# First chunk of the projections: q and k row tile by row tile in one loop, their last 64 rows side by side

## The chip, the cores and the metric

The kernel runs on one core of one Trainium2 chip. A core has five engines that run on their own and wait for one another by semaphores: TensorE (PE, matmuls; PEld is its weight load, which overlaps the matmuls), VectorE (DVE), ScalarE (ACT), GpSimd (POOL) and SyncE (SP), which here issues the DMA transfers. Each engine runs its own instructions in the order in which they were written. Matmuls accumulate in PSUM banks; other data lie in SBUF, 128 partitions wide. The metric is the device time of one execution in microseconds (us). The profiled execution is a single one with the hardware profiler on; its rows give the start and length of each instruction in us from the start of the span.

## The reference

One sequence of S = 2048 tokens with D = 448 features goes through two branches, which a gate mixes per token:

```python
x = A_x
g = _sigmoid((x * gate_w).sum(-1, keepdims=True))
a = _A_ref(x, A_wqkv, A_wo)                  # attention
b = _B_ref(x, B_w1, B_b1, B_w2, B_b2)        # relu(x @ w1 + b1)**2 @ w2 + b2
return g * a + (1 - g) * b
```

The attention has 16 heads of 28 features. Each token looks at eight keys, those 0, 2, ..., 14 places before it (`W, dil = 8, 2`), with a softmax over the eight; q, k and v are the three thirds of `x @ wqkv`. All data are float32. Only the first projections, `x @ wqkv` for a quarter of the tokens, are touched by the change.

## The kernel before, in words

**Precision by three products.** TensorE works on a shortened float32 (`fp32r`). Each operand is therefore split into a high part, rounded by a copy on ACT, and a low part, the rest, by a subtraction on DVE (`split_full`, lines 113 to 115). A product is the sum of three matmuls: high by high, high by low, low by high.

**Tiling.** The 448 rows of the contraction are three row tiles of 128 and a last one of 64 (`w7h`, `w7l`, `x.x7`, `x.x8` hold the last one; it stands in both halves of the partitions, the upper half of its weights being q's and the lower half k's). A chunk is 512 tokens, four token tiles of 128. An accumulator (`Acc`) is one PSUM bank with 128 tokens by 448 columns (450 for q, whose columns 448 and 449 are the gate's). It needs 9 full matmuls (three row tiles by three products) and three half matmuls for the last 64 rows. Alternatively a full matmul can be cut into two halves of 64 rows; `side_by_side` issues two such halves, of two different accumulators, on the two halves of the array, and a pair takes as long as one full matmul. An accumulator that goes from one half of the array to the other needs a small write to its bank in between, a turn, by DVE or ACT (`turn`, lines 191 to 199).

**Banks.** There are eight PSUM banks, four under the tag "b" and four under "m", each tag given out in rotation. In the first chunk q's four accumulators take the "b" banks, k's the "m" banks, and v's again the "b" banks.

**The first chunk, `qkv_first` (line 257).** Before the change it does, in this order on TensorE: for each of the three row tiles the 12 full matmuls of q (3 products, 4 token tiles); then 48 pairs of halves, in which q's last 64 rows run beside k's last 64 rows (12 pairs) and then k's full row tiles run as halves of two token tiles (36 pairs); then v in 42 pairs. Between the pairs stand turns and evacuations. A call of `run` takes two lists of halves and a list of steps (up to which pair, which accumulators are then complete, which turns).

**Evacuation, `qkv_evacuate` (line 201).** ACT copies the bank into a stage tile in SBUF (line 207). A stage tile holds two neighbouring token tiles of one of q, k or v; the pool has `ST_BUFS = 3` of them in rotation under one tag. When the second half is in, SP stores the stage tile to DRAM with one DMA of 448 KB (line 213). For q, ACT also copies the gate's column (line 215). A stage buffer can be given out again when its store is complete.

**Loads at the start (lines 635 to 652).** SP issues, for each row tile, q's weights and x; then the last 64 rows; then k's three row tiles and v's. Each row tile is split on ACT and DVE (lines 653 to 667), first q's weights and x, then the last 64 rows, then k's weights (lines 711 and 712).

**The order of the rest.** The kernel is written in one order by hand. A model clock (`advance`, `at`, `when`) counts the planned time of the matmuls that were emitted, and emits work that falls due: v's weight splits at 12,000 ns and after, the store of the split x to DRAM (`x_spill`, line 139) at 10,500, the splits of chunk 1's x from 19,000, the next x loads, and so on. In what order such work and the evacuations stand on ACT, DVE and SP follows from how far the clock was moved at that point. The next chunks use `qkv_two`; attention on POOL, DVE and ACT and the second branch follow.

Of the kernel before, what the change touches and what calls it, by code (L numbers as in the profile page):

```python
# [7 lines left out]
F32 = mybir.dt.float32  # L8
# [5 lines left out]
S, D, H, DH, W, F = 2048, 448, 16, 28, 8, 1792  # L14
P = 128
# [8 lines left out]
NQ = D + 2  # L24
# [7 lines left out]
MM448 = 203.0  # L32
# [25 lines left out]
def gated_mix_kernel(ctx: ExitStack, tc: tile.TileContext, xT, wqkv, w1, w2, wo, b1, b2, out):  # L58
    nc = tc.nc

    def f32(ap):
        return ap.bitcast(F32)
# [29 lines left out]
    attp = ctx.enter_context(tc.tile_pool(name="attp", bufs=1))  # L92
# [20 lines left out]
    def split_full(raw, hi, lo, soon=now):  # L113
        nc.scalar.activation(hi, raw, AF.Copy)
        soon(lambda: nc.vector.tensor_sub(lo, raw, f32(hi)))

    def split_x78(raw, x7, x8, soon=now):

        split_full(raw, x7, x8, soon)
# [12 lines left out]
    def x_tiles(c, pool):  # L132
        return X([pool.tile([P, 2, CH], F32R, tag=f"x{j}", name=f"x{c}_{j}") for j in range(4)])
# [19 lines left out]
    wqh = ap.tile([P, 3, NP + 2 * D], F32R, name="wqh")  # L153
    wql = ap.tile([P, 3, NP + 2 * D], F32R, name="wql")
# [10 lines left out]
    def ncols(b):  # L165
        return NQ if b == 0 else D

    def block(b):

        o = (0, NP, NP + D)[b]  # L170
        return slice(o, o + ncols(b))
# [8 lines left out]
    def side_by_side(*todo):  # L180


        assert len(todo[0]) == len(todo[1])
        for pair in zip(*todo):
            for r, (acc, a, w) in enumerate(pair):
                rows = slice(r * 64, r * 64 + 64)
                assert acc.rows in (None, r)
                nc.tensor.matmul(acc.pt[:, :acc.n], a[rows], w[rows], start=acc.todo == acc.all, stop=acc.todo == 1)  # L188
                acc.todo, acc.rows = acc.todo - 1, r

    def turn(one, two):


        for acc in (one, two) if one is not two else (one,):
            if one is two:
                nc.scalar.activation(acc.pt[0:1, 511:512], none, AF.Copy)
            else:
                nc.vector.memset(acc.pt[0:1, 511:512], 0.0)
            acc.rows = None
# [17 lines left out]
    def full(x, acc, tl, b, ks=range(3)):  # L217
        sl, n = slice(tl * P, tl * P + P), block(b)
        r = []
        for k in ks:  # L220
            r += [(acc, x.h[k][:, sl], wqh[:, k, n]), (acc, x.h[k][:, sl], wql[:, k, n]),
                  (acc, x.l[k][:, sl], wqh[:, k, n])]
        return r

    def last(x, acc, tl, b):

        sl = slice(tl * P, tl * P + P)
        n = block(1) if b == 2 else slice(0, ncols(b))
        h, l = w7h[:, n], w7l[:, n]
        return [(acc, x.x7[:, sl], h), (acc, x.x7[:, sl], l), (acc, x.x8[:, sl], h)]  # L230

    def accs(c, b, tls, tags):
        return [Acc(t, f"qkv{c}_{tl}_{b}", ncols(b)) for t, tl in zip(tags, tls)]

    def run(c, todo, steps):


        a = 0
        for e, done, *turns in steps:
            side_by_side(todo[0][a:e], todo[1][a:e])  # L240
            while a < e:
                n = min(12, e - a)
                if clock["on"] and a + n == e:

                    advance(max(n - LEAD, 0) * MM448)
                    while turns and not callable(turns[0]):
                        turn(*turns.pop(0))
                    n = min(n, LEAD)
                advance(n * MM448)
                a = min(a + 12, e)  # L250
            for t in turns:
                t() if callable(t) else turn(*t)
            for b, tl, acc in done:
                assert acc.todo == 0
                qkv_evacuate(acc.pt, c, tl, b)

    def qkv_first(x):


        four = range(4)  # L260
        q = accs(0, 0, four, "bbbb")
        for k in range(3):
            for two in ((0, 1), (2, 3)):
                for j, prods in enumerate(zip(*(full(x, q[i], i, 0, (k,)) for i in two))):
                    for acc, a, w in prods:
                        nc.tensor.matmul(acc.pt[:, :NQ], a, w, start=k == j == 0, stop=False)  # L266
            advance(12 * MM448)
        for acc in q:
            acc.todo = 3
        k = accs(0, 1, four, "mmmm")  # L270
        t = [sum((last(x, a[i], i, b) for i in four), []) for b, a in ((0, q), (1, k))]
        f = [full(x, k[i], i, 1) for i in four]
        run(0, [t[0] + f[0] + f[1] + f[2] + f[3], t[1] + f[2] + f[3] + f[0] + f[1]],
            [(3, [(0, 0, q[0])], (k[0], k[0])),
             (12, [(0, i, q[i]) for i in (1, 2, 3)], (k[1], k[1])),
             (24, [], (k[0], k[2])), (33, [], (k[1], k[3])),
             (39, [(1, 0, k[0]), (1, 2, k[2])]), (48, [(1, 1, k[1]), (1, 3, k[3])])])
        v = accs(0, 2, four, "bbbb")
        f, l = [full(x, v[i], i, 2) for i in four], [last(x, v[i], i, 2) for i in four]
        run(0, [f[0] + l[0] + f[2] + l[2] + f[1] + f[3], f[1] + l[1] + f[3] + l[3] + f[0] + f[2]],  # L280
            [(15, [], (v[0], v[1])), (24, [], (v[2], v[3])),
             (33, [(2, 0, v[0]), (2, 1, v[1])]), (42, [(2, 2, v[2]), (2, 3, v[3])])])
# [192 lines left out]
    def soon(fn):  # L475
        at(LO_DELAY, fn)

    def advance(dt):
        clock["pe"] += dt
        while due := [x for x in later if x[0] <= clock["pe"]]:  # L480
            item = min(due, key=lambda x: x[0])
            later.remove(item)
            item[1]()
        if not clock["on"]:
            clock["att"] = clock["pe"]
            return
        while clock["att"] < clock["pe"]:
            try:
                r = next(att)
            except StopIteration:  # L490
                clock["on"] = False
                return
            if r is None:
                clock["att"] = clock["pe"]
                return
            clock["att"] += r


    def raw_tile(name):
        return rawp.tile([P, 4, 512], F32, tag="raw", name=name)  # L500
# [90 lines left out]
    def h_first(x, c, f):  # L591

        accs = [Acc("m", f"h{c}_{f + r}", CH) for r in range(2)]
        go([h_last(x, a, f) + h_full(x, a, f + r, (0, 1, 2)) for r, a in enumerate(accs)], MM512)
        return accs
# [37 lines left out]


    raws = [raw_tile("wqraw0")]
    rx = raw_tile("xraw0")
    for k in range(4):
        if k < 3:
# [3 lines left out]
                nc.sync.dma_start(raws[0][rows, k, :NQ], wqkv[b, rows, k])  # L642
        for cols in ((slice(0, 256), slice(256, CH)) if k == 0 else (slice(0, CH),)):
            nc.sync.dma_start(rx[:, k, cols], xT[0, :, k, cols])

    for b, tag in ((1, "k"), (2, "v")):
        raw = attp.tile([P, 3, D], F32, tag=tag, name=f"wqraw{b}")
        for k in range(3):
            nc.sync.dma_start(raw[:, k], wqkv[b, :, k, :D])
        raws.append(raw)  # L650
    raw7 = attp.tile([P, D], F32, tag="q", name="wqraw7")
    nc.sync.dma_start(raw7, wqkv[2, :, 3, :D])
    x = x_tiles(0, xap)
    for k in range(3):
        nc.scalar.activation(wqh[:, k, :NQ], raws[0][:, k, :NQ], AF.Copy)
        halves = (slice(0, 256), slice(256, CH))
        for i, cols in enumerate(halves):

            if k == i == 0:
                nc.vector.tensor_copy(x.h[k][:, cols], rx[:, k, cols])  # L660
            else:
                nc.scalar.activation(x.h[k][:, cols], rx[:, k, cols], AF.Copy)
        nc.vector.tensor_sub(wql[:, k, :NQ], raws[0][:, k, :NQ], f32(wqh[:, k, :NQ]))
        for cols in halves:
            nc.vector.tensor_sub(x.l[k][:, cols], rx[:, k, cols], f32(x.h[k][:, cols]))
    split_full(raws[0][:, 3, :NQ], w7h[:, :NQ], w7l[:, :NQ])
    split_x78(rx[:, 3], x.x7, x.x8)

    def wq_split(b, k):
        if k < 3:  # L670
            split_full(raws[b][:, k], wqh[:, k, block(b)], wql[:, k, block(b)])
        else:
            split_full(raw7, w7h[:, NP:], w7l[:, NP:])
# [34 lines left out]
        nc.sync.dma_start(b1t, b1)  # L708
        nc.sync.dma_start(b2t, b2.partition_broadcast(P))

    for k in range(3):
        wq_split(1, k)
    for k in range(4):
        when(12000.0 + k * 900.0, wq_split, 2, k)
    for c, t in SPLIT_AT.items():
# [31 lines left out]
    for c in range(4):  # L747
        x = xs[c]
# [291 lines left out]
    c, x = ORDER[0], xm[3]  # L1040
# [8 lines left out]
    for g in range(2, 2 * NF):  # L1049
        i, f = g // (NF // 2), g % (NF // 2) * 2  # L1050
# [3 lines left out]
        last = g == 2 * NF - 1  # L1054
        if not f:
            x, slots = X([nxt[j][0] for j in range(4)]), [nxt[j][1] for j in range(4)]
            nxt = {}
        hold[0] = ends
        accs = h_first(x, c, f)
# [110 lines left out]
```

## Time and profile before

| | us |
|---|---|
| median of 3 runs | 414.65 (414.2 to 414.75) |
| the profiled execution: its time | 414.58 |
| its span, first to last instruction | 412.7 |
| TensorE busy | 408.4 |
| GpSimd busy | 268.6 |
| VectorE busy | 255.9 |
| ScalarE busy | 211.9 |
| DMA, mean over the span | 179 GB/s |

How to read the rows that follow. A row of the timeline has the start in us, the length in us, the engine (SPq is SyncE's queue of DMA issues), the line of the kernel, the operation, what is written from what, shapes, and the count of like instructions merged in the row; in brackets stands how long the engine was idle before it and what ended that idle time. A row of waits has who waited for whom, the total, the times, and the longest. A row of windows has the stretch, then for PE, PEld, DVE, ACT and POOL the busy time and instruction count, the granted TensorE clock, the DMA share and GB/s. A row of DMA issues has the count, the size of each and the median time from issue to landing. Where a row speaks of a tile "landing us min/median/max", these are its stores from issue to landing. Matmuls are pipelined, so the lengths of neighbouring ones overlap; the distance of their starts is the pace.

### The profile page before, as it was taken

What the parts mean: (1) busy time and instruction counts of PE and PEld (TensorE: products, weight loads), DVE (VectorE), ACT (ScalarE), POOL (GpSimd) and SP (SyncE); (2) the same over time, 40 slices, a digit from 0 to 9 for tenths busy, and PEclk for the clock granted to TensorE, in tenths of its full rate; (3) what the DMA queues carried; (4) which work ended last, traced back from release to release, by engine and by line L of the source; (5) the groups of instructions that cost most, each with busy time, mean ns of one, the idle gap of its engine ahead of it and who ended that gap; (6) DMA issues with size and microseconds to landing.
All of it is one profiled execution on the core that took longest, in us unless ns stands there. A gap on an engine that the chain in (4) does not pass through costs nothing.

```text
span 412.7 us, 9323 instructions
## 1 busy us (share of the span) xinstructions
PE 408.4 (99%) x3835; PEld 377.6 (91%) x3835; DVE 255.9 (62%) x404; ACT 211.9 (51%) x477; POOL 268.6 (65%) x167
## 2 busy tenths in 40 slices
PE   8999999999999999999999999999999999999997
PEld 8999999999999999888888888989898888888996
DVE  4520523276767767777656798879576677892354
ACT  5642556378756565444565535444653254346540
POOL 0000000965989999999989899999899977860000
PEclk9999999999999999999999999999999999999999
DMA  7989799989164307654112649765145611168204
GB/s 236 380 318 326 227 364 292 363 259 321 47 224 159 128 2 258 207 186 152 37 50 93 233 157 266 200 149 149 24 163 192 224 46 59 72 175 139 91 0 180
DMA packets 65611, 73.76 MB, mean 179 GB/s; under 512 B 32352, under 2 KB 58528, under 8 KB 65184
## 3 DMA queue, kind: packets, MB, share of 16 engines
q1 hardware_dynamic: 65568, 73.16, 54.5%
q8 instruction: 30, 0.49, 0.5%
q14 instruction: 13, 0.11, 0.1%
HBM read 45.71 MB, written 28.25 MB: 179 GB/s over the span
## 4 chain that ended last, share of the span: by engine, by line
PE 99%; DVE 0%; issue 0%
PE b L188 33%; PE h L188 32%; PE qkv L188 23%; PE a L188 7%; PE qkv L266 2%; PE warm L632 1%; PE a L944 1%; PE last L944 0%; DVE bt L823 0%; PE last L936 0%; PE a L936 0%; DVE zero L629 0%; DVE b1z L630 0%
## 5 line engine op out<-in xcount | busy, mean ns | idle before, releaser
L339 POOL TENSOR_TENSOR qk<-q,k 128x896 f32<-128x896 f32 x64 | 135.0, 2138 | 83.2 <-DMA k<-k_d 78.9
L346 POOL TENSOR_TENSOR av<-lg,v 128x896 f32<-128x896 f32 x64 | 119.5, 1962 | 8.0 <-DVE lg L340 5.6
L188 PE MATMUL qkv<-wqh,x 64*128 64x448 f32 (+1 forms) x528 | 90.9, 360 | 0.0
L619 DVE TENSOR_TENSOR h<-h,h 128x512 fp32r<-128x512 f32 x56 | 38.3, 687 | 60.8 <-ACT h L622 60.4
L188 PEld LDWEIGHTS qkv<-wqh,x 64*128 64x128 f32 x528 | 74.0, 184 | 1.3
L188 PE MATMUL qkv<-wql,x 64*128 64x448 f32 (+1 forms) x264 | 74.7, 360 | 0.0
L188 PE MATMUL b<-w2ah,h 64*128 64x448 f32 x448 | 70.4, 359 | 0.0
L188 PE MATMUL b<-w2bh,h 64*128 64x448 f32 x448 | 69.6, 360 | 0.0
L340 DVE TENSOR_REDUCE lg<-qk 128x32 f32<-128x896 f32 x64 | 67.1, 1076 | 2.2 <-POOL qk L339 2.1
L354 DVE TENSOR_REDUCE o<-av 128x112 f32<-128x896 f32 x64 | 66.5, 1070 | 2.1 <-POOL av L346 1.8
L620 ACT ACTIVATE h<-h,b1z 128x512 f32<-128x512 f32 x56 | 36.7, 656 | 44.0 <-PE h L188 44.0
L188 PEld LDWEIGHTS b<-w2ah,h 64*128 64x128 f32 x448 | 48.0, 184 | 2.8
L188 PEld LDWEIGHTS b<-w2bh,h 64*128 64x128 f32 x448 | 46.0, 184 | 3.2 <-ACT h L571 0.3
L188 PE MATMUL b<-w2al,h 64*128 64x448 f32 x224 | 47.6, 358 | 0.0
L188 PEld LDWEIGHTS qkv<-wql,x 64*128 64x128 f32 x264 | 45.5, 184 | 0.7
L188 PE MATMUL b<-w2bl,h 64*128 64x448 f32 x224 | 45.8, 358 | 0.0
L207 ACT ACTIVATE st<-qkv 128x448 f32<-128x448 f32 x48 | 24.5, 543 | 32.2 <-PE qkv L188 27.1
L188 PE MATMUL h<-x,w1h 64*128 64x512 f32 x168 | 36.1, 386 | 0.0
L621 ACT ACTIVATE h<-h 128x512 fp32r<-128x512 f32 x56 | 33.5, 599 | 1.7
L622 ACT ACTIVATE h<-h 128x512 f32<-128x512 f32 x56 | 33.2, 593 | 0.0
L188 PE MATMUL h<-x,w1l 64*128 64x512 f32 x84 | 29.7, 386 | 0.0
L571 ACT ACTIVATE h<-h 128x4 fp32r<-128x4 f32 (+1 forms) x35 | 7.2, 206 | 42.6 <-PE b L188 42.4
(145 smaller groups left out, 749.4 us busy)
## 6 DMA issues: line engine op xcount, KB each, us to landing
k<-k_d SPq DMA_DIRECT2D x8, 840.0 KB, 6.7
v<-v_d SPq DMA_DIRECT2D x8, 840.0 KB, 4.4
x_d<-x SPq DMA_DIRECT2D x11, 512.0 KB, 6.0
q_d<-st SPq DMA_DIRECT2D x8, 448.0 KB, 4.6
k_d<-st SPq DMA_DIRECT2D x8, 448.0 KB, 4.1
v_d<-st SPq DMA_DIRECT2D x8, 448.0 KB, 7.1
w1raw<-w SPq DMA_DIRECT2D x4, 896.0 KB, 10.0
q<-q_d SPq DMA_DIRECT2D x8, 448.0 KB, 3.6
```

The costliest lines, as they stand in the source:

```text
L188: nc.tensor.matmul(acc.pt[:, :acc.n], a[rows], w[rows], start=acc.todo == acc.all, stop=acc.todo == 1)
L207: nc.scalar.activation(st[:, :, t % 2], pt[:, :D].rearrange("p (g c) -> p g c", g=G), AF.Copy)
L266: nc.tensor.matmul(acc.pt[:, :NQ], a, w, start=k == j == 0, stop=False)
L339: nc.gpsimd.tensor_mul(pr, q[:, s:s + 1].to_broadcast([P, W, C]), k[:, s:s + W])
L340: pending.append(lambda: nc.vector.tensor_reduce(lg[:, s], pr.rearrange("p w (h d) -> p w h d", h=HG), axis=AX.X, op=ALU.add))
L346: nc.gpsimd.tensor_mul(pr.rearrange("p (h d) w -> p w h d", h=HG), lg[:, s][:, :, :, None].to_broadcast([P, W, HG, DH]), v[:, s:s + W].rea ...
L354: nc.vector.tensor_reduce(o[:, g * C:(g + 1) * C], pr, axis=AX.X, op=ALU.add)
L571: nc.scalar.activation(ap, f32(ap), AF.Copy)
L619: nc.vector.tensor_sub(hl, pt, f32(hh))
L620: ops += [lambda pt=pt, r=r: nc.scalar.activation(pt, pt, AF.Relu, bias=b1t[:, f + r:f + r + 1]), lambda pt=pt, hh=hh: nc.scalar.activatio ...
L621: lambda pt=pt, hh=hh: nc.scalar.activation(hh, pt, AF.Square),
L622: lambda pt=pt, r=r, low=low: (nc.scalar.activation(pt, pt, AF.Square), at(delays[r], low))]
```

## The change

In the code, `qkv_first` takes q's and k's eight accumulators at once. For each row tile it issues q's 12 full matmuls and then k's 12 full matmuls, moving the model clock by 12 matmuls after each. Then the last 64 rows of q and k run side by side in 12 pairs, and after each three pairs q's and k's token tile are evacuated, one after the other. The turns of k's accumulators and k's halves are gone. v follows as before.

The load of k's row tile r is issued behind the r-th load of x instead of behind the last 64 rows, and its split stands behind the r-th split of x. The raw tiles of k's and v's weights are allocated ahead of x's. Everything else is as it was; the number of stage tiles too.

```diff
-        q = accs(0, 0, four, "bbbb")
-        for k in range(3):
-            for two in ((0, 1), (2, 3)):
-                for j, prods in enumerate(zip(*(full(x, q[i], i, 0, (k,)) for i in two))):
-                    for acc, a, w in prods:
-                        nc.tensor.matmul(acc.pt[:, :NQ], a, w, start=k == j == 0, stop=False)
-            advance(12 * MM448)
-        for acc in q:
+        q, k = accs(0, 0, four, "bbbb"), accs(0, 1, four, "mmmm")
+        for r in range(3):
+            for b, tiles in ((0, q), (1, k)):
+                for two in ((0, 1), (2, 3)):
+                    for j, prods in enumerate(zip(*(full(x, tiles[i], i, b, (r,)) for i in two))):
+                        for acc, a, w in prods:
+                            nc.tensor.matmul(acc.pt[:, :acc.n], a, w, start=r == j == 0, stop=False)
+                advance(12 * MM448)
+        for acc in q + k:
             acc.todo = 3
-        k = accs(0, 1, four, "mmmm")
-        t = [sum((last(x, a[i], i, b) for i in four), []) for b, a in ((0, q), (1, k))]
-        f = [full(x, k[i], i, 1) for i in four]
-        run(0, [t[0] + f[0] + f[1] + f[2] + f[3], t[1] + f[2] + f[3] + f[0] + f[1]],
-            [(3, [(0, 0, q[0])], (k[0], k[0])),
-             (12, [(0, i, q[i]) for i in (1, 2, 3)], (k[1], k[1])),
-             (24, [], (k[0], k[2])), (33, [], (k[1], k[3])),
-             (39, [(1, 0, k[0]), (1, 2, k[2])]), (48, [(1, 1, k[1]), (1, 3, k[3])])])
+        run(0, [sum((last(x, tiles[i], i, b) for i in four), []) for b, tiles in ((0, q), (1, k))],
+            [(3 * i + 3, [(0, i, q[i]), (1, i, k[i])]) for i in four])
...
     raws = [raw_tile("wqraw0")]
+
+    for b, tag in ((1, "k"), (2, "v")):
+        raws.append(attp.tile([P, 3, D], F32, tag=tag, name=f"wqraw{b}"))
...
             nc.sync.dma_start(rx[:, k, cols], xT[0, :, k, cols])
-
-    for b, tag in ((1, "k"), (2, "v")):
-        raw = attp.tile([P, 3, D], F32, tag=tag, name=f"wqraw{b}")
-        for k in range(3):
-            nc.sync.dma_start(raw[:, k], wqkv[b, :, k, :D])
-        raws.append(raw)
+        if k < 3:
+            nc.sync.dma_start(raws[1][:, k], wqkv[1, :, k, :D])
+    for k in range(3):
+        nc.sync.dma_start(raws[2][:, k], wqkv[2, :, k, :D])
...
             nc.vector.tensor_sub(x.l[k][:, cols], rx[:, k, cols], f32(x.h[k][:, cols]))
+        split_full(raws[1][:, k], wqh[:, k, block(1)], wql[:, k, block(1)])
...
-    for k in range(3):
-        wq_split(1, k)
```

## The prediction

> **What bounds the kernel now.** I read the page's busy shares first, then what TensorE waited for, then the first 31 us instruction by instruction.
>
> ```profile
> span 412.7 us, 9323 instructions
> PE 408.4 (99%) x3835; PEld 377.6 (91%) x3835; DVE 255.9 (62%) x404; ACT 211.9 (51%) x477; POOL 268.6 (65%) x167
> ...
> PE warm L632 <- DVE b1z L630: 1.2, 1, 1.2
> ...
> PEld a L944 <- issue: 0.3, 1, 0.3
> PEld qkv L188 <- ACT wqh L114: 0.3, 1, 0.3
> ...
> 31.00:100.00 69.00, 69.00 (x687) 66.99 (x685) 26.35 (x80) 40.01 (x94) 19.25 (x10) 1.00 0.92 308
> ```
>
> TensorE (PE) is the bound from 1.2 us to the end, and after the start it waits for nobody. From 31 to 100 us it runs 687 matmuls in 69.00 us, two 64-row halves per 0.2 us, without a hole. So a hole that an edit makes or fills in the first chunk goes into the total at full size: there is no later wait that could absorb it.
>
> The question is then what holes the first chunk has today. A busy PE is modelled, so I go by the starts.
>
> ```profile
> 4.13 1.03 PE L266 MATMUL qkv<-wqh,x 128*128 128x450 f32 x2
> ...
> 7.39 0.96 PE L266 MATMUL qkv<-wqh,x 128*128 128x450 f32 x4
> ...
> 12.20 0.56 PE L266 MATMUL qkv<-wqh,x 128*128 128x450 f32 x2
> 12.69 0.47 PE L188 MATMUL qkv<-w7h,x 64*128 64x450 f32 x2
> 13.00 0.37 PE L188 MATMUL qkv<-w7l,x 64*128 64x448 f32 x2
> ```
>
> Row tile 0 of q (12 matmuls from 4.13; its last two are the first two of the four at 7.39) runs slowly. From 7.79 the next 24 run at 0.2 us each: the pair at 12.20 and 12.40 is where 7.79 + 22 and 23 steps of 0.2 us put it. Data are therefore not late after 7.79, although q alone eats a row tile in 2.4 us. The only later hole is at the change from 128-row to 64-row matmuls: the first pair of halves is due at 12.60, starts at 12.69, and the second comes 0.31 us later instead of 0.2; 0.2 us are lost. The other such change, ahead of line 944, has the same 0.3 us of idle weight load, and waits for nothing there ("issue").
>
> **The change, part by part.** *TensorE's work.* Before: 36 full matmuls for q, then 48 pairs of halves. After: 72 full ones, then 12 pairs. Both are 84 steps of 0.2 us. Row tile 0 of q meets the same first loads in the same order, so its slow 3.66 us stay. The one change from 128 to 64 rows stays too, later. Its 0.2 us are saved only if they were a wait for the key splits, which the release named above allows; the row at line 944 speaks for the change of form itself. I take 0 (bounds -0.2 and 0). By steps: k's row tile 0 starts at 7.79, 60 steps later (19.79) the halves begin, first pair 19.88, second 20.19, the n-th 20.19 + 0.2 x (n - 2). The thirteenth step, v's first, falls at 22.39; today it is the second of the two pairs in this row, 22.41:
>
> ```profile
> 22.21 0.63 PE L188 MATMUL qkv<-wqh,x 64*128 64x448 f32 x4
> ```
>
> *Loads and splits.* The key loads move ahead of later q loads on SP's queue, and the key splits ahead of later q splits on ACT and DVE.
>
> ```profile
> 2.13 0.43 SPq L639 DMA_DIRECT2D wqraw<-wqkv  x1
> ...
> 6.18 0.58 ACT L655 ACTIVATE wqh<-wqraw 128x450 fp32r<-128x450 f32 x1 [0.23 <-DMA wqraw<-wqkv]
> 6.93 0.72 ACT L662 ACTIVATE x<-xraw 128x256 fp32r<-128x256 f32 x2 [0.17 <-DMA xraw<-xT]
> ...
> 8.86 0.72 ACT L662 ACTIVATE x<-xraw 128x256 fp32r<-128x256 f32 x2 [0.73 <-DMA xraw<-xT]
> ...
> 10.71 1.78 ACT L114 ACTIVATE wqh<-wqraw 128x448 fp32r<-128x448 f32 x3
> 10.93 0.33 SPq L565 DMA_DIRECT2D xraw<-xT  x1
> ```
>
> Key tile 0 takes the queue place of q's tile 1 (issued 2.13, in hand at 6.18): high part on ACT 6.18 to 6.76, low part on DVE about 0.6 us later, 7.4; wanted at 7.79 and 8.19. The next q tile takes the place that was in hand at 6.93 and is wanted at 10.19; key tile 1 the place of 8.86, wanted at 12.59. From there TensorE takes 4.8 us per row tile and the margin grows. Cost 0. If that cover went (key tile 0 late by d), d would be paid; 0.4 us are to spare. The last 64 rows are split behind 1.8 us of key splits, so the x load at 10.93, which needs their buffer, goes out near 12.7; its first reader today runs at 23.55.
>
> *Evacuation.* Here the change does something that the steps do not show. Today q's four evacuations run from about 14 us, k's from 20.88. After it all eight follow one another on ACT, two for each three pairs, and they need four stage tiles at once (q 0/1, k 0/1, q 2/3, k 2/3) where the pool has three. The fourth, asked for by k's tile 2, is the buffer of q 0/1, free only when its store has landed. ACT runs in order, and q's tile 3 stands right behind. Until that is copied out, v's tile 3 has no bank. Such a wait for a stage buffer exists today, once, harmless:
>
> ```profile
> 14.37 0.52 ACT L207 ACTIVATE st<-qkv 128x448 f32<-128x448 f32 x1
> 14.79 0.14 ACT L215 ACTIVATE zg<-qkv 128x1 f32<-128x1 f32 x1
> 14.84 0.55 ACT L207 ACTIVATE st<-qkv 128x448 f32<-128x448 f32 x1
> ...
> 14.91 1.49 SPq L213 DMA_DIRECT2D q_d<-st  x2
> ...
> 20.88 0.98 ACT L207 ACTIVATE st<-qkv 128x448 f32<-128x448 f32 x2 [2.95 <-PE qkv L188]
> ...
> 57.17 0.37 SPq L213 DMA_DIRECT2D k_d<-st  x1
> k_d<-st SPq DMA_DIRECT2D x1, 448.0 KB, 9.0
> 66.26 0.55 ACT L207 ACTIVATE st<-qkv 128x448 f32<-128x448 f32 x1 [0.44 <-DMA k_d<-st]
> ```
>
> The store issued at 57.17 landed 9.0 us later, 66.17, and ACT went on at 66.26. Now the times. k's tile 0 was copied from 20.88, 0.48 us after its last pair began, the 39th (13.00 + 37 x 0.2 = 20.40). After the change the third pair starts at 20.39: q0 on ACT at 20.87; its gate column 0.42 later, 21.29; k0 0.05 behind, 21.34; the next 0.43 later (0.98 for two, less the last one's 0.55): q1 21.77 to 22.32, gate column 22.19 to 22.35, k1 22.24, q2 22.67, its column 23.09, k2 due at 23.14. The store of q 0/1 goes out 0.02 behind q1, 22.34 (14.89 to 14.91 in the rows).
>
> How long does that store take to land?
>
> ```profile
> DMA to landing us min/median/max: 3.7/5.8/9.4
> DMA to landing us min/median/max: 2.8/4.6/9.4
> k_d<-st SPq DMA_DIRECT2D x2, 448.0 KB, 4.1
> q_d<-st SPq DMA_DIRECT2D x1, 448.0 KB, 4.5
> ...
> 13.00:22.40 9.40, 9.40 (x96) 9.34 (x94) 2.73 (x9) 5.26 (x16) 0.00 (x0) 1.00 1.01 383
> ```
>
> Stores of stage tiles: 2.8 to 9.4 us over the whole run, least 3.7 in the first 70 us (the line with 3.7 is for that stretch), 4.1 for k's two of this chunk and 4.5 at 14.91. These two went out with the engines full. After the change the spill of x (four stores of 512 KB) goes out before the q stores instead of behind them, from about 13, behind the x load of 1 MB: 3.1 MB at 383 GB/s is 8 us, done by 21 or 22. So the store at 22.34 meets queues that are almost empty, and I take 3.7, bounds 2.8 and 9.4. By the Trainium skill (DMA: Bandwidth & Descriptors, Anatomy of one DMA) a transfer costs about 2.0 us fixed plus its bytes at 436 GB/s, which for 448 KB is an estimate of 3.05 us and a total of 416.5; the page fits it on another issue path, and two of the rows here are a good microsecond longer.
>
> With 3.7: landed 26.04, k2 on ACT at 26.13, q3 26.56, its gate column 26.98 to 27.13, v's tile 3 on TensorE 0.2 later, 27.33:
>
> ```profile
> 3.64 0.29 DVE L660 CAST x<-xraw 128x256 fp32r<-128x256 f32 x1 [2.50 <-DMA xraw<-xT]
> ```
>
> (the first split ends at 3.93, the first matmul of q starts at 4.13). Without the hole, tile 3 is due 12 steps into v. v's tile 1 needs q1's column, 22.35 + 0.2 = 22.55, against 22.39: 0.16 lost. Tile 3 is then due at 24.95: 27.33 - 24.95 = 2.38 lost.
>
> *What is late next.* Queued on ACT behind it: k3 at 27.03, then the four x splits of chunk 1, and on DVE the two markers that let v's tiles 0 and 1 change row halves:
>
> ```profile
> 23.55 2.19 ACT L114 ACTIVATE x<-xraw 128x512 fp32r<-128x512 f32 x4
> 24.21 1.93 DVE L115 TENSOR_TENSOR x<-xraw,x 128x512 fp32r<-128x512 f32 x3 [4.40 <-ACT x L114]
> 25.50 0.06 DVE L198 MEMSET qkv<- 1x1 f32 x2
> ```
>
> The split starts at 27.46, DVE 0.66 later, the markers are done 1.38 after that, 29.50, TensorE may go on at 29.70; it is due there 12 steps after 27.33, 29.73. A tie; I count 0 (bounds 0 and 0.2). Chunk 1's splits end near 30.7 and are wanted when v ends, 33.3. Stores and v's evacuations follow later by the same 2.5 us.
>
> **Sum:** 0 + 0.16 + 2.38 = 2.5 us. The profiled execution took 414.58 (span 412.7 and 1.88 around it; the median of the runs shown is 414.65): 414.58 + 2.5 = 417.1 us. In general the loss is the landing time less 1.2: 416.2 for 2.8, 417.5 for 4.1, 419.1 for the 5.7 us that a spill store takes here:
>
> ```profile
> x_d<-x SPq DMA_DIRECT2D x9, 512.0 KB, 5.7
> q_d<-st SPq DMA_DIRECT2D x1, 448.0 KB, 9.4
> ```
>
> **The rivals.** *TensorE comes back slow.* After the hole of 2.4 us it could run as at the start:
>
> ```profile
> 1.20 3.14 PE L632 MATMUL warm<-zero 128*128 128x256 f32 x13 [1.20 <-DVE b1z L630]
> 5.71 1.44 PE L266 MATMUL qkv<-wqh,x 128*128 128x450 f32 x4
> 6.99 0.57 PE L266 MATMUL qkv<-wql,x 128*128 128x450 f32 x2
> ```
>
> Thirteen matmuls of 256 columns in 3.14 us are 0.242 each, 0.42 for 448 columns against 0.2, and full pace is reached between 5.71 and 6.99, about 5 us after 1.20. Five microseconds at 0.42 do the work of 2.4: 2.6 more, 419.7. Against it: the hole is half as long as that stretch, and no hole in this trace shows such a drop. The Trainium skill (TensorE: Matmul & The Clock Gate, The HAM clock gate) gates the clock after an idle window of about 3.4 us; by that rule 2.4 us are too short, but a landing of 4.8 us or more would do. The granted clock in the trace reads 1.00 even in the slow first microseconds, so it could not tell. Chance 0.06.
>
> *The store lands late*, behind spills still in the queues, as the 9.4 us one did: 414.58 + 8.2 = 422.8. For it, the queues are full until 21 at least; against it, nothing is issued in the 4 us ahead of the store. Chance 0.06.
>
> *Not slower: the buffer is free before it matters.* With q 0/1 stored within 1.3 us, q3 is out in time and the hole is gone; with the 0.2 us of the change of form saved as well, 414.4. It decides at 1.3 us from issue to release. Against it stands the smallest landing of all, 2.8, and the row at 66.26, which shows that ACT waits for the landing and not for the read. A gain over 0.2% (0.83 us) would have to come from the slow first row tile besides, which nothing in the edit touches. Chance 0.07.
>
> **How the numbers follow.** The forecast has 0.81, with 416.0 (landing 2.8, and 0.2 saved) to 419.1. The range goes up to 419.8 to take in the slow restart; outside stay 0.06 and 0.07. About 0.2% is what a measurement of this kernel can tell from no change. Slower: 0.81 + 0.06 + 0.06 = 0.93; of the not-slower case 0.05 within 0.2% and 0.02 faster.
>
> **What would show it.** In the changed profile: TensorE at even steps from 7.8 to 19.8 (else a split is late); v starting near 22.4; one copy to the stage on ACT that waits 2 to 4 us for a DMA of q's stage; and right behind it TensorE's only hole, some 2.4 us, ending with q's tile 3 copied. I am wrong if that copy does not wait, if the hole is filled, or if matmuls after it start 0.42 apart.

## The result and the profile after

| | before | after |
|---|---|---|
| median, us | 414.75 (414.20 to 417.21, 5 runs) | 421.43 (419.33 to 421.67, 5 runs) |
| ratio | | 1.0143 (95% interval 1.0115 to 1.0170) |
| profiled execution, us | 414.58 | 421.61 |
| its span, us | 412.7 | 419.5 |
| mean granted TensorE clock in it | 1.000 | 0.992 |

The change makes the kernel 1.4% slower. Slower was forecast, at 417.1 us and at most 419.8; the loss is 6.7 us where 2.5 were expected. The five executions after the change lie 2.3 us apart, and their clocks go along: the quickest (419.33 us) had a mean granted clock of 0.999, the two slowest (421.61 and 421.67) 0.992. What follows reads the profiled execution, one of the two slowest.

First what TensorE waited for after the change, in the view of waits (total, times, longest):

```profile
span 419.5 us, 9243 instructions
...
PE qkv L188 <- ACT zg L215: 4.2, 1, 4.2
PE warm L627 <- DVE b1z L625: 1.2, 1, 1.2
PE qkv L267 <- ACT x L658: 0.6, 1, 0.6
```

There is one new wait that counts, on the copy of a gate column. The timeline around it, TensorE's rows, then ACT's, then SP's, then the landing of the two stores that go out at 22.25 and 29.26:

```profile
19.84 0.47 PE L188 MATMUL qkv<-w7h,x 64*128 64x450 f32 x2
...
22.35 0.46 PE L188 MATMUL qkv<-wqh,x 64*128 64x448 f32 x2
...
24.75 0.36 PE L188 MATMUL qkv<-wqh,x 64*128 64x448 f32 x1
...
29.35 0.74 PE L188 MATMUL qkv<-wqh,x 64*128 64x448 f32 x1 [4.24 <-ACT zg L215]
...
32.13 0.94 PE L188 MATMUL qkv<-wqh,x 64*128 64x448 f32 x2
32.51 0.94 PE L188 MATMUL qkv<-w7h,x 64*128 64x448 f32 x2
...
35.00 0.56 PE L188 MATMUL qkv<-wqh,x 64*128 64x448 f32 x2
22.14 1.03 ACT L207 ACTIVATE st<-qkv 128x448 f32<-128x448 f32 x2
22.98 0.24 ACT L215 ACTIVATE zg<-qkv 128x1 f32<-128x1 f32 x1
28.25 0.98 ACT L207 ACTIVATE st<-qkv 128x448 f32<-128x448 f32 x2 [5.03 <-DMA q_d<-st]
29.12 0.18 ACT L215 ACTIVATE zg<-qkv 128x1 f32<-128x1 f32 x1
...
22.25 0.37 SPq L213 DMA_DIRECT2D q_d<-st  x1
...
29.26 0.36 SPq L213 DMA_DIRECT2D q_d<-st  x1
q_d<-st SPq DMA_DIRECT2D x1, 448.0 KB, 5.9
q_d<-st SPq DMA_DIRECT2D x1, 448.0 KB, 2.8
```

Up to 24.75 the kernel does what was computed: the halves begin at 19.84 (19.88 forecast), v at 22.35 (22.39), q 0/1's store goes out at 22.25 (22.34). Then the fourth copy to a stage, k's tile 2, sits on ACT for 5.03 us until that store has landed; q's tile 3 comes behind it, and v's tile 3 behind that. The hole is 29.35 - 24.75 less the normal 0.20, 4.40 us; 2.38 were forecast. The store took 5.9 us to land instead of 3.7, while the next one, seven microseconds later with the queues empty, took 2.8.

The second half of the loss starts where the hole ends. Rows at 32.13 and 32.51 are one step apart: 0.38 us instead of 0.20. The windows show the clock (stretch, PE busy, granted clock, DMA share, GB/s):

```profile
24.80:29.35 4.55, 0.31 (x5) 0.85 0.52 181
29.35:32.00 2.65, 2.65 (x14) 0.50 0.69 229
32.00:35.00 3.00, 3.00 (x20) 0.53 1.01 317
35.00:36.00 1.00, 1.00 (x13) 1.00 0.92 385
```

It is 0.85 in the mean over the hole, so half speed for its last 1.4 us, from about 28.0, 3.0 us after TensorE ran out of work; and it stays at half until about 34.8 (0.53 over the three microseconds from 32 is half speed for 2.82), 5.5 us after work came back. Fifteen steps of 0.375 us fill the 5.65 us to 35.0; at 0.2 they take 3.0. The cost is 2.65 us. Together 4.40 + 2.65 = 7.05; 6.8 show in the span.

Why the store was late stands in the DMA windows of TensorE's view (last column GB/s), first two of the kernel before, then of the changed one, and the spill's four stores:

```profile
8.00:12.00 4.00, 4.00 (x22) 1.00 1.05 356
...
14.00:16.00 2.00, 2.00 (x22) 1.00 0.88 365
```

```profile
8.00:12.00 4.00, 4.00 (x22) 1.00 1.06 278
...
14.00:16.00 2.00, 2.00 (x12) 1.00 0.56 96
...
18.00:20.00 2.00, 2.00 (x12) 1.00 0.96 277
...
13.96 0.33 SPq L560 DMA_DIRECT2D xraw<-xT  x1
14.34 2.51 SPq L141 DMA_DIRECT2D x_d<-x  x4
x_d<-x SPq DMA_DIRECT2D x4, 512.0 KB, 9.8
```

The loads moved fewer bytes per microsecond, the next x load went out at 13.96 instead of the 12.7 forecast, the DMA engines were half idle from 14 to 16, and from 18 to 20 they moved 277 GB/s although they were busy; from 14 to 22 the mean is 278 GB/s. By 22.25 us 5.8 MB had been moved of the 6.7 MB (3.6 of loads, 1.0 of x, 2.1 of spill) that had to be gone; the other 0.9 MB stood ahead of the store. At 410 GB/s that is an estimated 2.2 us, and with the 2.8 of an empty queue 5.0 of the 5.9; where the rest went is not shown.

### The profile page after: what moved, and what is told of

Read it like the earlier page. It is cut to its first block, busy times and chain, and to the rows that moved or that the text cites. A ratio compares the mean times of both kernels' runs of the same rounds, so it can differ in the third digit from the quotient of the medians.

```text
span 419.5 us, 9243 instructions
## 1 busy us (share of the span) xinstructions
PE 410.4 (98%) x3799; PEld 379.8 (91%) x3799; DVE 255.3 (61%) x400; ACT 212.0 (51%) x475; POOL 268.4 (64%) x167
## 4 chain that ended last, share of the span: by engine, by line
PE 96%; DMA 2%; ACT 1%; SPq 0%; DVE 0%; issue 0%; ACTq 0%
PE b L188 32%; PE h L188 32%; PE qkv L188 20%; PE a L188 7%; PE qkv L267 3%; DMA q_d<-st 1%; DMA xraw<-xT 1%; PE a L939 1%; ACT st L207 1%; PE last L939 0%; DVE bt L818 0%; ACT x L658 0%; SPq L642 0%; SPq L637 0%; PE last L931 0%
## 5 line engine op out<-in xcount | busy, mean ns | idle before, releaser
L188 PE MATMUL qkv<-wqh,x 64*128 64x448 f32 (+1 forms) x480 | 83.8, 367 | 4.2 <-ACT zg L215 4.2
L188 PEld LDWEIGHTS qkv<-wqh,x 64*128 64x128 f32 x480 | 63.8, 189 | 5.2 <-ACT zg L215 4.6
L188 PE MATMUL b<-w2ah,h 64*128 64x448 f32 x448 | 67.6, 359 | 0.0
L188 PE MATMUL qkv<-wql,x 64*128 64x448 f32 (+1 forms) x240 | 60.7, 368 | 0.0
L188 PEld LDWEIGHTS b<-w2ah,h 64*128 64x128 f32 x448 | 43.8, 184 | 2.8
L188 PE MATMUL b<-w2al,h 64*128 64x448 f32 x224 | 41.8, 358 | 0.0
L188 PE MATMUL b<-w2bl,h 64*128 64x448 f32 x224 | 41.5, 359 | 0.0
L188 PEld LDWEIGHTS qkv<-wql,x 64*128 64x128 f32 x240 | 36.0, 189 | 0.3
L188 PE MATMUL h<-x,w1h 64*128 64x512 f32 x168 | 30.9, 386 | 0.0
L188 PE MATMUL h<-x1b,w1h 64*128 64x512 f32 x168 | 28.2, 387 | 0.0
```

## The experiments

**The hole is the wait for a stage buffer.** Two kernels give chunk 0 more stage tiles, in buffers that are free by then. The first puts only the fourth tile elsewhere:

```diff
-            stage[b, t // 2] = xap.tile([P, G, 2, C], F32, tag="stage", name=f"st{c}_{tl}_{b}", bufs=ST_BUFS)
+            if (c, b, tl) == (0, 1, 2):
+                stage[b, t // 2] = attp.tile([P, G, 2, C], F32, tag="k", name="st0_2_1")
+            else:
+                stage[b, t // 2] = xap.tile([P, G, 2, C], F32, tag="stage", name=f"st{c}_{tl}_{b}", bufs=ST_BUFS)
```

> Theory (the wait for the stage buffer is the loss, and the slow clock only follows from it): no copy to the stage waits for a DMA, v's tile 3 starts at its due step, the granted clock stays 1.00 after 7 us, and the time is that of the kernel before, 414.6 us (414.2 to 415.0). Rival (the earlier key loads and splits cost by themselves): the hole goes, but the time stays at 416 or above.

Measured 416.12 us (ratio 1.0030, 1.0018 to 1.0042), mean clock 0.999 to 1.000. The hole is gone and 5.3 us with it, but 1.3 stay, so by its time this run alone would speak for the rival. Only 0.3 of them lie in the span (medians 413.3 us against 413.0); the rest is time outside it, of which more at the end. In the profiled execution, with a span of 413.5, the trace shows TensorE's second wait and what ACT waited for shortly before:

```profile
49.78 0.36 PE L188 MATMUL qkv<-wqh,x 64*128 64x448 f32 x1
50.70 0.48 PE L188 MATMUL qkv<-wqh,x 64*128 64x448 f32 x2 [0.56 <-DVE qkv L198]
...
46.53 0.55 ACT L210 ACTIVATE st<-qkv 128x448 f32<-128x448 f32 x1 [4.68 <-DMA v_d<-st]
```

It is the same hazard one chunk later: with five instead of six tiles taken from the pool of three in chunk 0, the rotation stands one place off, and a copy of chunk 1 meets a store of v, issued at 37.05 us, that took 9.4 us to land.

The second kernel, the six-stage kernel from here on, therefore takes three tiles out of the rotation:

```diff
+            own = {(1, 2): "k", (2, 0): "q", (2, 2): "v"}.get((b, tl)) if c == 0 else None
+            if own:
+                stage[b, t // 2] = attp.tile([P, G, 2, C], F32, tag=own, name=f"st{c}_{tl}_{b}")
```

> The changed kernel with three stage tiles of chunk 0 (k 2/3, v 0/1, v 2/3) in buffers that are free by then, so that the three pool buffers are as far in their rotation as before at chunk 1. Theory (all that is lost is waits for stage buffers, in chunk 0 and, where the rotation was shifted by one, again near 50 us): no copy to the stage holds up TensorE anywhere, 414.4 to 415.0 us. Rival (the order itself costs 0.3%): 415.7 us or above, with no wait of TensorE on the stage.

Measured 415.29 us, ratio 1.0012 (1.0002 to 1.0021), span 413.1; TensorE's waits on this kernel in full:

```profile
PE warm L631 <- DVE b1z L629: 1.2, 1, 1.2
PE qkv L271 <- ACT x L662: 0.2, 1, 0.2
```

No wait on the stage is left, and the time is that of the kernel before to within the 0.2% that can be told, though 0.3 us over the forecast stretch; the median span is 413.0 us against 412.9. So the new order of the matmuls, by itself, is worth nothing and costs next to nothing, and the rival's 0.3% is not there.

**What stands behind the waiting copy pays.** Copying all four tiles of q ahead of k's frees v's banks in time:

```diff
-            [(3 * i + 3, [(0, i, q[i]), (1, i, k[i])]) for i in four])
+            [(3 * i + 3, [(0, i, q[i])]) for i in range(3)] + [(12, [(0, 3, q[3])] + [(1, i, k[i]) for i in four])])
```

> Theory (the wait stays with k's tile 2, and what stands behind it on ACT pays): q's tile 3 is out by 23.5 us and v's tile 3 starts on time; ACT still waits for the store of q 0/1 until about 27.5, chunk 1's x splits come after it, the two markers on DVE near 31, so TensorE waits at v's 25th pair, due at 27.2, for some 4 us, and the clock drops as well: 420 to 421.5 us. Rival (only v's bank matters): no hole, 414.6 us.

Measured 420.58 us, ratio 1.0143 (1.0126 to 1.0160), as slow as the change. The hole moved to where the theory put it, the markers of the row halves (last row, DVE):

```profile
27.34 0.37 PE L188 MATMUL qkv<-w7h,x 64*128 64x448 f32 x2
30.66 0.59 PE L188 MATMUL qkv<-wqh,x 64*128 64x448 f32 x2 [2.96 <-DVE qkv L198]
...
30.53 0.06 DVE L198 MEMSET qkv<- 1x1 f32 x2
```

TensorE's hole is 3.1 us, and the clock dropped here too, though only for 3.4 us (half speed for 1.13 us of the first window and for 0.28 of the last):

```profile
30.66:32.00 1.34, 1.34 (x8) 0.58 0.98 244
32.00:34.00 2.00, 2.00 (x12) 0.50 0.99 389
34.00:36.00 2.00, 2.00 (x22) 0.93 0.07 29
```

**The loads alone.** The loads and splits of the change with the matmul order of before:

> The loads and splits of the change with the matmul order of the kernel before. Theory (loads and splits cost nothing): no wait for a stage buffer, 414.6 us (414.2 to 415.0). Rival (key loads ahead of q's later tiles starve TensorE, or crowd the DMA queues): TensorE waits between 7.8 and 12.6 us, 415.5 us or above.

Measured 415.63 us, ratio 1.0024 (1.0013 to 1.0034). Here the rival has it: TensorE waits for the second row tile of x (and 0.4 us for the first, at 4.70).

```profile
7.05 0.58 PE L266 MATMUL qkv<-wqh,x 128*128 128x450 f32 x2
8.79 0.67 PE L266 MATMUL qkv<-wqh,x 128*128 128x450 f32 x2 [1.16 <-ACT x L663]
```

The key loads do push x back by over a microsecond; in the changed kernel k's 12 matmuls of row tile 0 run in that time. "Cost 0" was right of the two parts together, not of the loads.

**Why the store landed late.** All four spill stores behind the q and k stores:

```diff
-    when(10500.0, x_spill, 0, x)
+    when(17500.0, x_spill, 0, x)
```

> Theory (the store of q 0/1 landed late because the four spill stores of x stood ahead of it): with the spill behind it, the store lands in 2.8 to 3.7 us, the hole ahead of v's tile 3 is 1.6 to 2.5 us, too short for the slow clock, and the time is 416.2 to 417.1 us. Rival (the store is slow whatever stands ahead of it, or any hole makes TensorE slow): landing near 5.9 us or 0.37 us steps after the hole, time 419 us or above.

Measured 422.64 us, ratio 1.0183 (1.0164 to 1.0203): of the forecast the first half came true and the time did not. Landing, the hole of chunk 0, and two later holes:

```profile
q_d<-st SPq DMA_DIRECT2D x1, 448.0 KB, 2.8
...
27.07 0.47 PE L188 MATMUL qkv<-wqh,x 64*128 64x448 f32 x1 [1.18 <-ACT zg L215]
...
53.23 0.47 PE L188 MATMUL qkv<-wqh,x 64*128 64x448 f32 x1 [2.63 <-ACT st L207]
...
56.80 0.48 PE L188 MATMUL qkv<-wqh,x 64*128 64x448 f32 x2 [0.90 <-DVE qkv L198]
```

The store landed in 2.8 us, the hole shrank to 1.3 us, and the profiled execution kept a clock of 1.00; two of the other three had 0.994 and 0.996. But the 2 MB stood in the queues of the next chunk, where a copy to the stage waited again, and TensorE behind it. The three holes are 5.2 us of the 7.1 that the span is longer; TensorE was also 0.8 us behind before the first of them, and the rest is not located. Moving only two of the four:

```diff
-    when(10500.0, x_spill, 0, x)
+    when(10500.0, x_spill, 0, x, (0, 1))
+    when(17500.0, x_spill, 0, x, (2, 3))
```

> The changed kernel with two of the four spill stores of chunk 0 behind the q and k stores, so that 1 MB less stands ahead of the store of q 0/1. Theory (the store waits for what is still queued, about 1.5 MB at its issue): landing 3 to 3.7 us, hole 1.5 to 2.4 us, clock at or near 1.00, and less pushed into chunk 1 than with all four behind: 416.5 to 418 us. Rival (landing does not hang on the backlog): near 5.9 us, 421 us.

Measured 418.85 us, ratio 1.0100 (1.0085 to 1.0115), 0.85 over the forecast. The copy of k's tile 2 went on at 25.31 (store issued at 22.32), the hole was 1.4 us, the clock 0.998 to 1.000; a second hole of about 1 us came at 52 to 53 us, and part of the rest I did not locate. Both kernels show the same: with less queued ahead the store lands sooner, and part of what is pushed back is paid later.

**The slow steps behind the hole.** The changed kernel with the hole filled by matmuls whose results nobody uses:

```diff
+        spare = [ps("m", f"fill{r}") for r in range(2)]
+        def fill():
+            for _ in range(19):
+                for r, pt in enumerate(spare):
+                    rows = slice(r * 64, r * 64 + 64)
+                    nc.tensor.matmul(pt[:, :D], x.h[0][rows, :P], wqh[rows, 0, block(1)], start=True, stop=True)
...
-            [(15, [], (v[0], v[1])), (24, [], (v[2], v[3])),
+            [(12, [], fill), (15, [], (v[0], v[1])), (24, [], (v[2], v[3])),
```

> The changed kernel with 38 further half matmuls (19 steps of 0.2 us, 3.8 us) into two spare banks at the place of the hole; their results are not used. Theory (the 0.37 us steps after the hole are the clock, lowered for want of work): the copy of k's tile 2 waits as long as before, but the granted clock stays 1.00 and the steps behind are 0.2 us: about 2.6 us less than the changed kernel, 418.6 to 419.3 us. Rival (the slow steps come from something else that is late, as DMA traffic or ACT): still 0.37 us steps, 421.4 us.

Measured 418.86 us, ratio 1.0098 (1.0085 to 1.0111), 2.57 less than the changed kernel. The copy of k's tile 2 still waits for the store, 4.60 us instead of 5.03, and TensorE goes on with v near 29 us, yet at full pace (PE's rows, then the window of the slow steps):

```profile
24.77 4.06 PE L280 MATMUL fill<-wqh,x 64*128 64x448 f32 x38
...
29.86 0.75 PE L188 MATMUL qkv<-wqh,x 64*128 64x448 f32 x4
30.26 0.55 PE L188 MATMUL qkv<-wql,x 64*128 64x448 f32 x2
...
29.35:32.00 2.65, 2.65 (x29) 1.00 0.85 281
```

Some 0.4 of the gain may be the shorter wait of this execution; the steps of 0.2 us and the clock of 1.00 are the fill. The 0.375 us steps come from want of work: the transfers around them were the same, and more matmuls made the kernel faster.

**Holes of a set length.** On the six-stage kernel, n clearings of v's tile 3 on DVE ahead of its first matmul make a hole without a wait for DMA:

```diff
+        for _ in range(n):
+            nc.vector.memset(v[3].pt, 0.0)
```

> No wait for a stage buffer (the six stage tiles), but six clearings of v's tile 3 on DVE ahead of its first matmul, some 3 us, which leave TensorE a hole of about 2.4 us at the same place. Theory (a hole below some 3.2 us leaves the clock alone): steps of 0.2 us behind it, 417.0 us, the first forecast. Rival (any hole of this kind slows the clock): 419.6 us.

> As the short hole, with ten clearings, some 5 us, a hole of about 4.5 us with no DMA in it. Theory (the clock falls about 3 us into a hole and is back 5 to 6 us after its end): granted clock 0.5 from about 28 to 35 us, steps near 0.37 us, 421.5 to 422 us. Rival (the slow steps need the DMA traffic of the changed kernel): 419.2 us, steps of 0.2 us.

> The six stage tiles with thirteen clearings of v's tile 3 on DVE, 0.667 us each from 21.9 us, so the last ends near 30.4 us: a hole of TensorE of about 4.5 us that no DMA makes. Theory (want of work lowers the clock, the more surely the longer the hole): granted clock 0.5 for some microseconds from about 3 us into the hole, steps near 0.37 us for 5 to 6 us behind it, a mean clock of 0.992 to 0.995 in most executions, 421.5 to 422.5 us. Rival (the slow steps need the DMA wait of the changed kernel): clock 1.00, 420 us.

Neither of the first two made the hole it was meant to. Tile 3 was now the first of v to be used, so it took the first bank that came free: the clearings start at 21.9 us instead of 24, one each 0.667 us, and v's tile 1, on a later bank, cost 0.7 us. With six there was only that: 416.01 us (ratio 1.0037; 415.22 to 419.43), so the short hole of the forecast was not tested. With ten it was followed by a hole of 2.3 us; 419.47 us (ratio 1.0118, 1.0102 to 1.0134). The second hole's length is near the 2.38 us that I had forecast for the change. In the profiled execution it left the clock alone (418.27 us, 1.000); the other three had a mean clock of 0.996 (419.23 to 420.24 us) and spans 1.3 to 1.9 us longer. No trace shows their holes; if they were the same length, a hole of 2.3 us can already lower the clock. With thirteen, aimed with these numbers, the hole was 4.3 us: 422.17 us, ratio 1.0186 (1.0169 to 1.0203), clock 0.992 three times and 0.996 once.

```profile
25.41 0.36 PE L188 MATMUL qkv<-wqh,x 64*128 64x448 f32 x1
29.88 0.74 PE L188 MATMUL qkv<-wqh,x 64*128 64x448 f32 x1 [4.11 <-DVE qkv L279]
...
28.00:30.00 2.00, 0.12 (x2) 0.64 1.16 354
30.00:32.00 2.00, 2.00 (x12) 0.50 0.96 393
32.00:34.00 2.00, 2.00 (x14) 0.50 0.13 53
34.00:36.00 2.00, 2.00 (x16) 0.65 0.01 4
```

The clock falls about 3.0 us into the hole (0.64 over two microseconds is half speed for 1.44) and is back 5.5 us after its end, as in the changed kernel, without any wait for DMA.

Why the same kernel sometimes drops and sometimes does not can be read from the traces' record of clock changes, the list behind the clock in the windows. Half speed lasted from 28.02 to 34.85 us in the changed kernel, from 28.58 to 35.40 with thirteen clearings and from 30.87 to 34.28 with q's tiles out first: 6.83, 6.83 and 3.41 us. Each drop stands 23.89 us, seven times 3.41, behind the first entry of its record, full speed from 4.13, 4.68 and 6.98 us. So in these traces the clock changed only on a grid of 3.41 us, whose place differed from one execution to the next. The 3.41 us ahead of the three drops held 3.07, 2.97 and 3.12 us without work. The two longest holes that left a traced clock alone lie across two cells of this grid, two stretches of 3.41 us: 2.3 us with ten clearings, at most 1.2 in one cell, and 2.8 us near 52 us with all spill stores behind, at most 1.7. A mean clock of 0.996 fits one cell at half speed in some 418 us, 0.992 two. This is read off afterwards; no run was made to test it.

## Why the prediction was right or wrong

**Right: the bound, and that nothing is saved.** The even steps and their count of 84 came out, and the change of form at 19.84 and the start of v within 0.05 us. The 0.2 us at the change of form stayed, as the forecast took it. The six-stage kernel shows that without the wait the change is worth nothing.

**Right: the mechanism.** A fourth stage tile out of a pool of three, k's tile 2 behind the store of q 0/1, q's tile 3 behind it on ACT, v's tile 3 behind that: each link is in the trace in this order, and taking out the first, in the two kernels with more stage tiles, takes out the hole of chunk 0. The 0.16 us for v's tile 1 did not appear: q1's column was done at 22.3, ahead of the matmul. The tie at the markers was not tested in the changed kernel, since the slow clock put TensorE's own due time back; with q's tiles out first the markers decided.

**Wrong: one term of the sum.** The first step that failed is "the store at 22.34 meets queues that are almost empty, and I take 3.7". It measured 5.9. I took 383 GB/s, the rate of a full queue in the old order, from about 13 us; in the new order the x load went out at 13.96 and the mean from 14 to 22 was 278 GB/s. So 0.9 MB were still queued where I had counted none. With the spill stores moved away the landing was 2.8 us (all four) and at most 3.0 (two of them), which shows the spill ahead of the store to be the cause.

**Wrong: two rivals that were one.** The late landing alone would have stayed inside the range: 414.58 + (5.9 - 1.2) = 419.3 us. What took the profiled execution out of it is the slow clock behind the hole, which the sum put at nothing; in the median execution (421.43 us, span 418.3, mean clock 0.996) time outside the span adds to it. The late landing (0.06) and the slow restart (0.06) were priced apart, although the text itself said that a landing of 4.8 us or more would bring the slow clock. So the late case had to carry its price too: 419.3 + 2.6 = 421.9 us, against 421.6 measured for the profiled execution. That agreement is in part luck. The price was worked out from 5 us at 0.42 per step; the rows show 5.65 us at 0.375, and the two differences cancel to 2.65. And it is the price of two cells of the grid: the mean clocks of the other executions (0.992, 0.996, 0.995, 0.999) fit two, one, one and none. The prediction also held that the granted clock could not tell; it did, with 0.50 from 28.0 us on.

The Trainium skill (TensorE: Matmul & The Clock Gate, The HAM clock gate) has the clock fall after an idle window of about 3.4 us. In the traces it fell when the 3.41 us ahead of the drop held 2.97 to 3.12 us without work, so a hole a little shorter than 3.4 us was not safe here; the three executions with ten clearings and a mean clock of 0.996 hint at shorter ones, but no trace shows their holes. The Trainium skill's rule for one transfer (DMA: Bandwidth & Descriptors, Anatomy of one DMA), by which the prediction worked out 3.05 us as an estimate, is near the 2.8 us of a store that met empty queues; most of the rest of the 5.9 went to bytes queued ahead, which that rule does not count.

**Open.** The time outside the span was 1.7 to 1.9 us before and 2.1 to 3.1 in the five executions after. So of the 6.7 us between the medians about 1.2 lie outside the span. The same shows in the two kernels with more stage tiles: with all three moved, the median is 0.6 us above the kernel before while the median spans are 0.1 apart. What that time is, no run shows.

## What to carry to other kernels

When two streams of results that came one after the other are made to come together, count the buffers between the copy and the store: the copy that finds none waits for a whole DMA, and everything behind it on its in-order engine waits too, needed or not. Size such a wait by what is queued ahead of the store at its issue, with the pauses that the new order makes, not by the landing time of a quiet moment. And a hole of TensorE of about three microseconds or more can cost its length plus a slow stretch behind it (here up to 2.65 us, and not in every execution), so price the two as one.

## What the runs showed of the hardware that was not expected

- Idle TensorE: half clock about 3.0 us into a hole of 4.3 or 4.4 us, and full clock again only 5.5 us after work came back (3.6 us behind the hole of 3.1 us). Filling the hole with matmuls that nobody needed saved 2.57 us in the medians.
- In the traces the clock changed on a grid of 3.41 us whose place differed between executions: half speed lasted 3.41 or 6.83 us, behind cells with 2.97 to 3.12 us without work; holes of 2.3 and 2.8 us that lay across two cells had no effect.
- A store of 448 KB from SBUF landed in 2.8 us with empty queues and in 5.9 us with 0.9 MB ahead of it.
